# Two pieces of w1 asked for ahead of the first keys and values, instead of four, and two converted ahead of the first maximum, instead of three

## The chip, the cores and the metric

The kernel runs on one core of a Trainium2 chip. The core has five engines with queues of their own: TensorE (PE in the profile, its weight loads PEld), VectorE (DVE), ScalarE (ACT), GpSimd (POOL) and SyncE (SP, which here only asks for transfers). Transfers run on 16 DMA engines. The metric is the time of one execution on the device, in microseconds (us).

## What is computed

Block-sparse attention for 4 batches, 8 heads, 768 positions of 64 dimensions, and behind it a normalised feed-forward layer with a residual:

```
block, n_blocks = 32, 24
scores = scale * q @ k.T                       # per batch and head
mask: own block and its two neighbours, first and last block (as row or column), 3 sampled blocks a row
attn = softmax(where(mask, scores, -1e9)); attn_out = attn @ v
x = attn_out, heads side by side               # (4, 768, 512)
xn = (x - mean) / sqrt(var + 1e-6) * g_ln
out = x + relu(xn @ w_ch1) @ w_ch2             # 512 -> 2048 -> 512
```

The weights come in as bits of 64-bit floats. The kernel turns them into 32-bit floats with integer operations and then into pairs of 16-bit floats (high and low part).

## The kernel before

**Tiles, jobs, visits.** The rows of a batch are six tiles of 128 rows, taken in the order 1, 2, 3, 0, 4, 5. A job loads the keys and values of a tile (tile 0, which holds the edge blocks, has two jobs). Each job has visits: two for an ordinary tile, one for each half of the heads. Keys (`ks`) and values (`vs`) have two buffers each, used in turn by the jobs.

**Steps.** The program is written out step by step, and each engine runs its instructions in the order in which they are written. Step s holds the scores and the maxima of visit s (`scores`, `biggest`), the product with the values and the evictions of visit s - 1 (`attn_v`, `evict`), the exponentials of visit s (`softmax`), and a list of tasks: the transposes (`turn`), the loads of the next job at a job's first visit (`keys`, `values`), and whatever `at(step, ...)` has put there. The feed-forward layer (`ffn`) begins in step 4, spread between the tasks.

**Transfers.** SP asks for the small inputs, the queries, the keys and the part of the values that needs no gathering. Job 0's keys are one transfer for windows (L144) and twelve for sampled blocks (L153), which need the block ids in registers first. GpSimd asks for the gathered values (L192, four for an ordinary tile), for the weights (L413 for w1, L416 for w2) and for the outputs. It also copies the edge keys (L168). SP's requests reuse eight completion semaphores in turn, so that a request can wait for an earlier one's landing.

**Weights.** w1 comes in eight pieces, w2 in sixteen. A piece of w1 lands in one of four places, `raw1`, which lie in the storage of w2's results (`w2h`, `w2l`). `split_w1` converts it: three integer instructions on VectorE (L421, L423, L425) into one of four places `con1` (`stg0`, `stg1`, the ends of `hh` and `hl`), two on ScalarE (L433, L434), and the subtraction for the low part on GpSimd (L435). Behind the subtraction of pieces 0 to 3, GpSimd asks for pieces 4 to 7. `split_w2` and `low_w2` do the like for w2 from step 3 on, four pieces a step. The first w2 pieces land in the places that pieces 6 and 7 of w1 were converted in, so their request waits for those.

```
    def split_w1(i):
        split_w(raw1[i % 4], con1[i % 4], w1h[:, :, fs], w1l[:, :, fs], SW1)
...
        if i + 4 < 8:
            load_w1(i + 4, nc.gpsimd)
```

Of the kernel before, what the change touches and what calls it, by code (L numbers as in the profile page):

```python
# [25 lines left out]
def sparse_attention_moe(  # L26
# [13 lines left out]
    nc = tc.nc  # L40
# [132 lines left out]
    def values(job):  # L173
        src, vs = v[job.b], job.vs
        if job.kind == "D":
            nc.sync.dma_start(vs[:, 0:6, :], src[0 : 6 * P, :].rearrange("(c p) e -> p c e", p=P))
            return
        n = len(job.blocks)
        i0 = job.blocks[0]
        nc.sync.dma_start(vs[0:96, 1 : 2 * n : 2, :],  # L180
                          bass.AP(src.tensor, src.offset + (i0 - 1) * BLK * HV,
                                  [[HV, 96], [BLK * HV, n], [1, HV]]))
        runs = [(0, n, NB - 1)]
        if NB - 2 in job.blocks:
            k = job.blocks.index(NB - 2)
            runs = [(0, k, NB - 1), (k, k + 1, NB)]
        for lo, hi, blk in runs:
            nc.sync.dma_start(vs[96:128, 2 * lo + 1 : 2 * hi : 2, :],
                              bass.AP(src.tensor, src.offset + blk * BLK * HV,
                                      [[HV, BLK], [0, hi - lo], [1, HV]]))  # L190
        for gg, i in enumerate(job.blocks):
            nc.gpsimd.indirect_dma_start(  # L192
                out=vs[:, 2 * gg, :], out_offset=None, in_=src,
                in_offset=bass.IndirectOffsetOnAxis(ap=rows[:, i : i + 1], axis=0))
# [217 lines left out]
    def load_w1(i, dma):  # L412
        dma.dma_start(raw1[i % 4].bitcast(I32), w1[i].bitcast(I32))  # L413
# [23 lines left out]
    def split_w1(i):  # L437
        fs = slice(i * 256, (i + 1) * 256)
        split_w(raw1[i % 4], con1[i % 4], w1h[:, :, fs], w1l[:, :, fs], SW1)
        split[1, i] = s  # L440
        if i + 4 < 8:
            load_w1(i + 4, nc.gpsimd)
# [56 lines left out]
    def at(step, fn, *args):  # L499
        todo.setdefault(step, []).append((fn, args))  # L500
# [4 lines left out]
    nc.scalar.dma_start(bid, blocks)  # L505
    nc.scalar.dma_start(id_sb, eye)
    nc.scalar.dma_start(g_sb, g.to_broadcast([P, DM]))
    for i in range(4):
        load_w1(i, nc.gpsimd)
    nc.vector.memset(eps, 1e-6)  # L510
    nc.vector.memset(rf, 0.0)
# [2 lines left out]
        pass  # L514
    index_b()
    values(jobs[0])
    for i in range(3):
        split_w1(i)
    for i in range(3, 8):
        at((i - 3) // 2, split_w1, i)  # L520
    for i in range(4):
        at(2, load_w2, i, nc.gpsimd)
    for i in range(16):
# [132 lines left out]
```

## Time and profile before

| | |
|---|---|
| median of 3 runs | 779.08 us (777.71 to 780.2) |
| the profiled execution | 781.21 us |
| its span, first to last instruction | 779.3 us |
| TensorE busy | 702.4 us, 90% |
| VectorE busy | 326.2 us, 42% |
| ScalarE busy | 271.9 us, 35% |
| GpSimd busy | 188.1 us, 24% |
| mean granted clock of TensorE, of full speed | 0.965 |
| moved by DMA | 132.16 MB, 170 GB/s in the mean |

The shares are means over a program with a beginning that is unlike the rest. In the page's forty slices of 19.5 us each, TensorE's busy tenths run 0445767 and stay at 9 from there to the last but one, while the DMA tenths run 8989872 in the first seven. Times below are counted from the span's start.

### The profile page before, as it was taken

The page shows a single profiled execution, that of the slowest core. Times are in us where ns is not written, and L with a number is a line of the kernel's source. Part 1 is how long each engine was busy: PE and PEld are TensorE (multiplying, and loading weights), DVE is VectorE, ACT ScalarE, POOL GpSimd, SP SyncE. Part 2 cuts the span into 40 slices and gives each one's busy share as a digit, 9 for nine tenths or more (in the row PEclk, how much of TensorE's full clock was granted, in tenths as well). Part 3 has the DMA queues.
Part 4 walks back from the last instruction along what each step waited for, and adds up shares of the span by engine and source line. Part 5 has one row for each costly group of instructions (what it writes and reads, how often), then busy time and mean ns, then how long its engine had stood idle before and what let it go on. Part 6 is the DMA issues. An engine that isn't in the chain of part 4 may idle for free.

```text
span 779.3 us, 21817 instructions
## 1 busy us (share of the span) xinstructions
PE 702.4 (90%) x9344; PEld 475.1 (61%) x9344; DVE 326.2 (42%) x658; ACT 271.9 (35%) x561; POOL 188.1 (24%) x220
## 2 busy tenths in 40 slices
PE   0445767999999999999999999999999999999997
PEld 0122653775775775865875856765856857757764
DVE  7577887343351333443432323444332333432211
ACT  2355344343342331443341523343423423342200
POOL 5565211133322203113421103115221012210000
PEclk9967877999999999999999999999999999999999
DMA  8989872767947355569855437379864247431000
GB/s 330 341 251 282 285 247 84 219 184 209 246 131 188 94 167 150 155 165 238 231 153 137 126 129 218 111 194 252 214 167 132 64 147 223 147 87 29 14 29 14
DMA packets 109792, 132.16 MB, mean 170 GB/s; under 512 B 34560, under 2 KB 80896, under 8 KB 108672
## 3 DMA queue, kind: packets, MB, share of 16 engines
q1 hardware_dynamic: 96848, 83.92, 40.5%
q0 software_dynamic: 12416, 46.51, 17.9%
q8 instruction: 74, 1.21, 0.7%
q10 hardware_dynamic: 432, 0.34, 0.1%
q14 instruction: 22, 0.18, 0.1%
HBM read 118.15 MB, written 6.29 MB: 160 GB/s over the span
## 4 chain that ended last, share of the span: by engine, by line
PE 71%; issue 13%; DMA 8%; DVE 5%; POOL 1%; SPq 1%; ACT 1%; POOLq 0%; DVEq 0%
PE pu L367 27%; PE pd L392 25%; PE ps L203 7%; PE pv L274 7%; PE pt L264 6%; DMA ks<-kT 5%; DMA vs<-v 3%; DVE ot L423 1%; DVE w2l L445 1%; DVE ot L421 1%; DMA samp<-sampled 1%; POOL xl L344 0%; DVE st L239 0%; DVE ot L425 0%; SPq L149 0%
## 5 line engine op out<-in xcount | busy, mean ns | idle before, releaser
L367 PEld LDWEIGHTS <-w1h 128*128 128x128 f16 x1664 | 153.6, 99 | 18.1 <-issue 0.2
L252 ACT ACTIVATE p<-ps,st 128x256 f32<-128x256 f32 (+1 forms) x208 | 85.9, 491 | 222.8 <-DVE rs L316 116.4
L392 PE MATMUL pd<-w2h,hl 128*128 128x512 f16 x384 | 147.0, 383 | 0.0
L392 PE MATMUL pd<-w2l,hh 128*128 128x512 f16 x384 | 147.0, 383 | 0.0
L392 PE MATMUL pd<-w2h,hh 128*128 128x512 f16 x384 | 146.9, 383 | 0.0
L378 DVE SCALAR_TENSOR_TENSOR hl<-pu,hh 128x512 f16<-128x512 f32 x96 | 66.4, 692 | 171.2 <-ACT hh L377 170.7
L392 PEld LDWEIGHTS <-hh 128*128 128x128 f16 x768 | 75.2, 99 | 84.7 <-issue 3.0
L367 PE MATMUL pu<-xth,w1h 128*128 128x256 f16 (+1 forms) x832 | 120.9, 267 | 0.0
L367 PE MATMUL pu<-xth,w1l 128*128 128x256 f16 (+1 forms) x832 | 120.9, 267 | 0.0
L367 PE MATMUL pu<-xtl,w1h 128*128 128x256 f16 (+1 forms) x832 | 120.8, 267 | 0.0
L203 PE MATMUL ps<-ks,q 64*32 64x256 f32 (+1 forms) x1664 | 73.5, 418 | 40.3 <-DMA ks<-kT 37.6
L239 DVE TENSOR_REDUCE st<-ps 128x4 f32<-128x1024 f32 (+1 forms) x60 | 69.0, 1151 | 93.5 <-PE ps L203 93.4
L192 POOL DMA_INDIRECT vs<-v,rows x88 | 86.9, 987 | 88.0 <-PE pv L274 49.4
L377 ACT ACTIVATE hh<-pu 128x512 f16<-128x512 f32 x96 | 57.5, 599 | 108.9 <-PE pu L367 108.5
L264 PE MATMUL pt<-id_sb,p 128*128 128x128 f32 x448 | 66.3, 289 | 27.3 <-ACT p L252 23.3
L398 DVE SCALAR_TENSOR_TENSOR ot<-pd,x 128x512 f32<-128x512 f32 x24 | 16.6, 690 | 160.3 <-PE pd L392 160.3
L367 PEld LDWEIGHTS <-w1l 128*128 128x128 f16 x832 | 78.5, 99 | 8.2
L265 ACT COPY pt<-pt 128x512 f32<-128x512 f32 x120 | 61.9, 564 | 61.2 <-PE pt L264 50.7
L264 PEld LDWEIGHTS pt<-id_sb,p 128*128 128x128 f32 x448 | 53.6, 147 | 39.2 <-ACT p L252 28.0
L274 PEld LDWEIGHTS pv<-vs,pt 128*32 128x32 f32 x3584 | 55.6, 110 | 33.9 <-issue 28.4
L400 POOL DMA_DIRECT2D out<-ot x24 | 14.0, 583 | 255.9 <-DVE ot L398 255.9
L203 PEld LDWEIGHTS ps<-ks,q 64*32 64x32 f32 x1664 | 27.1, 109 | 72.0 <-issue 37.1
(83 smaller groups left out, 454.0 us busy)
## 6 DMA issues: line engine op xcount, KB each, us to landing
ks<-kT SPq DMA_DIRECT2D x28, 768.0 KB
ks<-kT SPq DMA_DIRECT2D x264, 64.0 KB
vs<-v SPq DMA_DIRECT2D x20, 780.0 KB
vs<-v SPq DMA_DIRECT2D x4, 1560.0 KB
q<-qT SPq DMA_DIRECT2D x24, 256.0 KB
out<-ot POOLq DMA_DIRECT2D x24, 256.0 KB
vs<-v SPq DMA_DIRECT2D x16, 260.0 KB
w2h<-w POOLq DMA_DIRECT2D x4, 1024.0 KB
```

Source lines behind the costliest of these rows:

```text
L192: nc.gpsimd.indirect_dma_start(out=vs[:, 2 * gg, :], out_offset=None, in_=src, in_offset=bass.IndirectOffsetOnAxis(ap=rows[:, i : i + 1], ...
L203: nc.tensor.matmul(ps[32 * part : 32 * part + 32, col : col + n], lhs[64 * row : 64 * row + 64], rhs[64 * row : 64 * row + 64], start=True ...
L239: nc.vector.tensor_reduce(out=st[:, 0:n], in_=seen(vi), axis=AX.X, op=ALU.max, negate=True)
L252: nc.scalar.activation(p_s[:, h * w : (h + 1) * w], seen(vi)[:, h, :], AF.Exp, bias=vi.st[:, 4 + h : 5 + h], scale=0.125)
L264: nc.tensor.transpose(pt[:, k - lo, :], p_s[:, k * P : (k + 1) * P], id_sb)
L265: nc.scalar.copy(dst[:, lo:hi, :], pt[:, 0 : hi - lo, :])
L274: nc.tensor.matmul(pv[32 * row : 32 * row + 32, 65 * col : 65 * col + 65], pt[:, ch, 32 * row : 32 * row + 32], vs[:, vv, 65 * e : 65 * e ...
L367: nc.tensor.matmul(ph[:, j * n : (j + 1) * n], w[:, ct, fs], x[:, ct, 0:n], start=m == 0, stop=m == 3 * CT - 1, skip_group_check=True)
L377: nc.scalar.activation(dh, ph, AF.Relu)
L378: nc.vector.scalar_tensor_tensor(out=dl, in0=ph, scalar=0.0, in1=dh, op0=ALU.max, op1=ALU.subtract)
L392: nc.tensor.matmul(po, x[:, f, ts], w[:, f, :], start=m == 0, stop=m == 3 * FT - 1)
L398: nc.vector.scalar_tensor_tensor(out=ot, in0=po, scalar=1.0 / (SW1 * SW2), in1=t.x, op0=ALU.mult, op1=ALU.add)
```

## The change

Of the four pieces of w1 that GpSimd asked for first of all, it now asks for two there and for the other two behind the loads of job 0's values. Two pieces are converted ahead of step 0 instead of three, and the conversions of pieces 2 to 7 are spread as 2, 3 in step 0, 4, 5 in step 1 and 6, 7 in step 2, where they were 3, 4 in step 0, 5, 6 in step 1 and 7 in step 2.

```
-    for i in range(4):
+    for i in range(2):
         load_w1(i, nc.gpsimd)
     nc.vector.memset(eps, 1e-6)
     nc.vector.memset(rf, 0.0)
...
     index_b()
     values(jobs[0])
-    for i in range(3):
+    for i in range(2, 4):
+        load_w1(i, nc.gpsimd)
+    for i in range(2):
         split_w1(i)
-    for i in range(3, 8):
-        at((i - 3) // 2, split_w1, i)
+    for i in range(2, 8):
+        at((i - 2) // 2, split_w1, i)
```

On GpSimd, at the program's start: `L413` asks for a piece of w1, `L168` copies edge keys into job 0's buffer, `L192` gathers job 0's values, `L435` is the subtraction of a piece.

```order
 L413 DMA w2h<-w 128x2048 x2
-L413 DMA w2l<-w 128x2048 x2
 L168 COPY ks_79<-kg_81 128x4x128 x2
 L192 DMA vs_83<-v,rows 128x520 x4
+L413 DMA w2l<-w 128x2048 x2
 L435 ISA
 L435 TENSOR_TENSOR w1l<-stg_108,w1h 128x4x256
```

The requests for pieces 2 and 3 went behind the four gathers of job 0's values. The rows of SP's queue are the same as before.

On VectorE, between step 1 and step 2: the three rows on `hh` are piece 6, those on `stg_109` ahead of them end piece 5; `L239` and `L240` are the maxima of the third visit, `L316` to `L322` the evictions of the second.

```order
 L425 SCALAR_TENSOR_TENSOR stg_109<-w2h,stg_109 128x1024
+L239 TENSOR_REDUCE st_417<-ps_400 128x4
+L240 TENSOR_SCALAR st_417<-st_417 128x4
+L316 TENSOR_SCALAR rs_453<-pv_420 128x4
+L318 RECIPROCAL rs_453<-rs_453 128x4
+L322 TENSOR_TENSOR x_90<-pv_420,rs_453 128x256
 L421 TENSOR_SCALAR hh<-w2l 128x1024
 L423 SCALAR_TENSOR_TENSOR hh<-w2l,hh 128x1024
 L425 SCALAR_TENSOR_TENSOR hh<-w2l,hh 128x1024
-L239 TENSOR_REDUCE st_423<-ps_406 128x4
-L240 TENSOR_SCALAR st_423<-st_423 128x4
```

Piece 6 went from ahead of the third maxima to behind the second visit's evictions; piece 7 (on `hl`) follows it there.

On GpSimd at the same place: `L435` on `hh` and `hl` are the subtractions of pieces 6 and 7, `L168` and `L192` belong to job 2, and `L416` is the first request for w2.

```order
 L435 TENSOR_TENSOR w1l<-stg_109,w1h 128x4x256
-L435 TENSOR_TENSOR w1l<-hh,w1h 128x4x256
 L168 COPY ks_79<-kg_81 128x4x128 x2
 L192 DMA vs_83<-v,rows 128x520 x4
+L435 TENSOR_TENSOR w1l<-hh,w1h 128x4x256
 L435 TENSOR_TENSOR w1l<-hl,w1h 128x4x256
 L416 DMA hh<-w 128x1024
```

Piece 6's subtraction went behind job 2's copies and gathers, next to piece 7's.

## Rows read from the trace of the kernel before

**Rows 1.** Busy us by stretch: PE, PEld, DVE, ACT, POOL, clock, DMA share, GB/s.
```profile
4.00:28.00 24.00, 2.70 (x12) 0.64 (x12) 18.84 (x33) 6.30 (x6) 12.75 (x11) 1.00 1.03 392
28.00:49.00 21.00, 8.90 (x132) 5.36 (x132) 15.90 (x18) 10.21 (x17) 12.01 (x11) 0.84 1.07 295
49.00:60.00 11.00, 6.55 (x109) 3.11 (x111) 5.69 (x9) 5.51 (x9) 8.14 (x6) 0.68 0.68 217
...
72.00:132.00 60.00, 38.74 (x611) 27.29 (x611) 51.97 (x92) 23.13 (x46) 10.42 (x17) 0.78 0.71 221
132.00:779.00 647.00, 638.39 (x8373) 434.97 (x8373) 226.95 (x496) 218.25 (x471) 134.85 (x160) 0.99 0.54 150
```
**Rows 2.** TensorE's waits, 80 to 140 us: total us, times, longest.
```profile
PE pt L264 <- ACT p L252: 17.5, 3, 9.2
```
**Rows 3.** Timeline of VectorE: start, us, line, tiles, idle before and its releaser.
```profile
32.72 1.23 DVE L239 TENSOR_REDUCE st<-ps 128x4 f32<-128x1024 f32 x1 [8.25 <-PE ps L203]
...
48.11 0.69 DVE L421 TENSOR_SCALAR hh<-w2l 128x1024 int32<-128x1024 int32 x1
...
48.83 1.23 DVE L423 SCALAR_TENSOR_TENSOR hh<-w2l,hh 128x1024 int32<-128x1024 int32 x1
...
50.09 1.23 DVE L425 SCALAR_TENSOR_TENSOR hh<-w2l,hh 128x1024 int32<-128x1024 int32 x1
...
58.53 0.68 DVE L421 TENSOR_SCALAR hl<-w2l 128x1024 int32<-128x1024 int32 x1
...
72.14 0.43 DVE L421 TENSOR_SCALAR ot<-hh 128x512 int32<-128x512 int32 x1 [5.13 <-DMA hh<-w]
```
**Rows 4.** The chain of waits, 0 to 84 us: start, us, what.
```profile
28.29 21.23 DMA vs<-v
...
52.41 4.01 PE ps L203 x32
```
**Rows 5.** Timeline of GpSimd.
```profile
2.53 1.06 POOL L413 DMA_DIRECT2D w2l<-w  x2
...
15.92 0.95 POOL L192 DMA_INDIRECT vs<-v,rows  x1 [0.30 <-issue]
...
42.35 0.59 POOL L413 DMA_DIRECT2D w2l<-w  x1
...
64.12 2.13 POOL L435 TENSOR_TENSOR w1l<-hl,w1h 128x1024 f16<-128x1024 f32 x1 [1.49 <-ACT w1h L434]
...
66.19 0.59 POOL L416 DMA_DIRECT2D hh<-w  x1
```
**Rows 6.** The page's DMA requests: count and KB of each.
```profile
ks<-kT SPq DMA_DIRECT2D x28, 768.0 KB
...
vs<-v SPq DMA_DIRECT2D x20, 780.0 KB
...
w2h<-w POOLq DMA_DIRECT2D x4, 1024.0 KB
```
**Rows 7.** DMA queues, 12 to 16 us (q0 GpSimd's, q1 SP's): packets, MB, share.
```profile
q0 software_dynamic: 187, 1.40, 82.8%
q1 hardware_dynamic: 189, 0.29, 19.2%
```
**Rows 8.** DMA queues, 28 to 32 us.
```profile
q1 hardware_dynamic: 588, 0.99, 105.5%
```
**Rows 9.** DMA queues, 36 to 40 us.
```profile
q0 software_dynamic: 263, 1.16, 73.1%
q1 hardware_dynamic: 269, 0.41, 28.4%
```
**Rows 10.** Timeline of TensorE: the scores of visit 0, last wait for keys.
```profile
30.00 1.92 PE L203 MATMUL ps<-ks,q 64*32 64x256 f32 x20 [2.47 <-DMA ks<-kT]
```
**Rows 11.** DMA queues, 48 to 50 us.
```profile
q0 software_dynamic: 90, 0.74, 91.6%
q1 hardware_dynamic: 104, 0.06, 11.6%
```

## The prediction

> **What bounds the kernel now.** I read the busy shares by stretch first, then the chain of waits of the first 84 us, then engine timelines around the places of the change, and last the DMA queues. [rows 1] split the program in two. From 132 us TensorE is busy 638.39 of 647.00 us: nothing that the change touches runs there, so a shift at 132 us arrives at the end as it is. From 72 to 132 us VectorE is busy 51.97 of 60.00 us, converting w2 in the order of its queue, and TensorE waits for it each step: three waits of the transposes for the exponentials cost 17.5 us [rows 2]. So a shift of the first w2 conversion, which starts at 72.14 us after 5.13 us of waiting for its transfer [rows 3], passes through as well. Before 60 us no engine is full, but the DMA share is 1.03 from 4 to 28 us and 1.07 from 28 to 49 us [rows 1]: the transfers are the bound. The chain [rows 4] names which: job 1's values, asked for at 28.29 us, are the last thing to land, 21.23 us later at 49.52 us. Their landing lets SP ask for the last of job 1's keys (its requests reuse completion semaphores, so one waits for an earlier one), and then come the scores of the third visit, until 56.42 us.
>
> So the time of the end is, in order: job 1's last key; the scores behind it; VectorE's third maximum and the second visit's evictions; the conversions of w1 queued behind those; the first w2 transfer; the w2 conversions. I call the first of these T, and ask two things: how far T moves, and what moves between T and 72.14 us.
>
> **First part: pieces 2 and 3 leave the front of the queue.** Before, GpSimd asks for the third and fourth piece at 2.53 us; the change puts them behind the indirect loads of job 0's values, whose last is asked for at 15.92 us and takes 0.95 us [rows 5]; so they are asked for at about 17. A piece is 1,024 KB, 1.05 MB [rows 6]. What a piece costs the keys is seen in the queue rows. From 12 to 16 us GpSimd's queue moved 187 packets and 1.40 MB, SP's 189 packets and 0.29 MB [rows 7]: packet for packet, so SP, whose rows are short, gets 0.07 MB per us beside 0.35. Alone SP moves 0.99 MB in 4 us, 0.25 per us [rows 8]. Beside a mixture with the indirect loads, whose rows are short too, it is 0.41 against 1.16 MB in 4 us, 0.10 and 0.29 per us [rows 9].
>
> With these rates I lay out the queues anew (an estimate from the rows named). Two pieces, 2.1 MB at 0.35, are through 6 us after the first packets at some 4 to 5 us; I take 11 us. Up to job 0's last key SP has to move 2.04 MB (72, 128 and 256 KB of small inputs, 768 KB of keys [rows 6], and twelve blocks of 128x128 floats, 64 KB each); some 0.6 are done by 11 us. The four indirect loads (each 128 rows of 520 floats, 1.06 MB together) take 3.7 us at 0.29, with 0.37 MB of SP's beside them; the other 1.1 MB go at 0.25, in 4.3 us. Job 0's keys are in at 19 us, where TensorE's last wait for them now ends at 30.00 us [rows 10]. That is 11 us, but not 11 us of T: VectorE's 8.25 us of waiting before the first maximum [rows 3] disappear with it, and nothing on the path hangs on either.
>
> From 19 us SP has to move job 0's values, the next queries, job 1's edge and window keys and its values: 2 x 1.065 + 0.262 + 0.786 = 3.18 MB, with 780 KB and 768 KB from [rows 6], the rest from the shapes. GpSimd's queue has pieces 2 to 5 (4.2 MB at 0.35: until 31), job 1's indirect loads (1.06 at 0.29: until 34.7), pieces 6 and 7 (2.1 at 0.35: until 40.7; VectorE has converted pieces 2 and 3, 3.2 us each, by about 29, so they are asked for in time). In these 21.7 us SP gets 18 x 0.07 + 3.7 x 0.10 = 1.63 MB; the other 1.55 go alone, in 6.2 us. Job 1's values land at 46.9 us instead of 49.5: **-2.6 us**.
>
> Behind them comes a tail of small keys. It now runs into piece 7, asked for at 42.35 us [rows 5], of which 90 packets and 0.74 MB pass between 48 and 50 us while the keys get 0.06 MB [rows 11]. In the new layout piece 7 is through by then. Those 2 us moved 0.06 MB of SP's, which alone take 0.3 us; but the last five requests are paced by their own issue, so I take **-1.0** of the possible 1.7. T moves by -3.6 us.
>
> Bounds for T. At one end every byte that stood ahead of T still does, and the share is already full: 0. At the other, the 21 us from 28 to 49 run at 295 GB/s where those before run at 392 [rows 1], because SP's queue is then mostly alone. If all of it ran mixed at 392, the stretch would shrink by 21 x (1 - 295/392) = 5.2 us, with 1.7 for the tail: -6.9. I take -3.6, since the layout still has SP alone for 6 us.
>
> The Trainium skill (DMA: Bandwidth & Descriptors, "Issuing engines are not separate DMA queues") says that requests of all engines run on the same 16 DMA engines and interleave. By that rule alone, on a share of 1.0, reordering would give T nothing; the 295 against 392 GB/s of this trace say that the mixture matters.
>
> **Second part: conversions move by half a step.** Pieces 2 to 6 change places with the maxima. For pieces 2 to 5 this costs nothing: they end before T, under VectorE's waits for keys, and in the new layout all four are done by about 37 us. Piece 6 is different. Now it is converted in step 1, ahead of the third maximum: 48.11, 48.83 and 50.09 us, 3.2 us from start to end on VectorE [rows 3], wholly under the wait for job 1's keys. Afterwards it stands in step 2, behind the evictions that follow those keys and ahead of piece 7, which starts at 58.53 us now [rows 3]. Queued behind it are piece 7, the norm, the fourth maximum; on GpSimd, piece 7's subtraction at 64.12 us and, at 66.19 us, the request for the first piece of w2 [rows 5], for which VectorE waits until 72.14. ScalarE and GpSimd take 2.1 us for a piece each and follow VectorE, so each of these is late by VectorE's 3.2 us. The transfer itself, 5.95 us from request to first use, I leave as it is: it gets clear of some of job 2's keys, and runs into the transposes instead. **+3.2 us**, from 2.2 (a quicker transfer) to 4.2 (the transposes and GpSimd beside VectorE). The norm and its transposes are late by 3.2 us too, but are used only after job 2's scores; job 2's keys have less beside them and are earlier. The w2 conversions still stand ahead of the fifth maximum on VectorE, so earlier keys give nothing back there.
>
> **Sum.** -2.6 - 1.0 + 3.2 = -0.4 us. The profiled execution took 781.21 us, span 779.3 and 1.9 around it; it would become 780.8. The median of the runs shown is 779.08, 2.1 lower; the same step from there gives **778.7 us**.
>
> **Rivals.** A measurement of this kernel can tell about 0.3% from no change, 2.3 us; below, "same" is 776.7 to 781.4.
>
> Slower: T does not move, because the 16 engines are full from 4 to 49 us and pieces 6 and 7 now pass entirely ahead of job 1's values. For it: shares of 1.03 and 1.07. Against it: the two rates of [rows 1]. Then only the 3.2 us of piece 6 are left: 782.3 us. It decides from the point where T gains less than 0.9 us. Chance 0.22. The skill's rule above leads here.
>
> Faster by mixing: job 1's values run beside the weights at more than 0.07 MB per us, as SP did with 0.10 in [rows 9]; T moves by up to 6.9 and the end by -3.7: 775.4 us. For it: the rate of values beside w1 rows is not in this trace, which has only keys there. Against it: one packet for one in every mixed window. Chance 0.16.
>
> Faster by cover: piece 6 is hidden after all, because the w2 transfer is quicker by as much once job 2's keys are through. Then -3.6 stands alone: 775.5 us. For it: VectorE waits 5.13 us for that transfer now. Against it: the request itself is late, behind piece 7 on GpSimd. Chance 0.10.
>
> The forecast, a gain of T eaten by piece 6, has 0.52, with its own range from 776.7 to 781.4. Faster is 0.16 + 0.10 = 0.26, slower 0.22. The range takes in most of both sides: 775.3 to 782.5.
>
> **What would show it.** TensorE's last wait for job 0's keys ends near 19 us and the first maximum starts near 21. The chain's transfer of job 1's values ends near 47, and the third visit's scores end near 53 instead of 56.42. Piece 6's three instructions stand behind the second visit's evictions, about 55 us, with piece 7 after them. The first w2 request is at about 66 and its first conversion within 1 us of 72.14. Everything behind keeps its distances. The prediction is wrong if job 1's values land at 49 or later, or before 45, or if the distance from the third scores to the first w2 conversion (15.7 us now) grows by less than 2 or more than 4.5 us.

## The result and the profile after

| | before | after |
|---|---|---|
| median | 779.08 us | 784.84 us (783.58 to 786.39, 5 runs) |
| ratio, 95% interval | | 1.0068 [1.0051, 1.0086] |
| the profiled execution, its span | 781.21, 779.3 us | 785.08, 783.2 us |
| TensorE, VectorE, ScalarE, GpSimd busy | 702.4, 326.2, 271.9, 188.1 us | 700.0, 322.4, 272.2, 188.6 us |
| mean granted clock | 0.965 | 0.954 |

The kernel became slower by 0.68%, 5.3 us. 778.7 us was forecast, with a range to 782.5: the forecast was wrong. No engine has noticeably more to do (the largest rise is 0.5 us, on GpSimd), so the time is waiting.

Busy time by stretch of the changed kernel, with the columns of [rows 1]:

```profile
4.00:28.00 24.00, 6.96 (x48) 3.03 (x56) 13.18 (x32) 6.67 (x10) 16.04 (x17) 1.00 1.03 319
28.00:49.00 21.00, 4.67 (x104) 2.94 (x88) 16.95 (x17) 11.37 (x15) 10.98 (x8) 0.61 1.03 357
49.00:60.00 11.00, 2.86 (x25) 0.96 (x30) 0.00 (x0) 0.00 (x0) 2.73 (x3) 0.50 0.68 170
72.00:132.00 60.00, 37.62 (x553) 27.23 (x553) 48.51 (x85) 25.84 (x51) 16.59 (x24) 0.76 0.77 252
132.00:783.00 651.00, 640.88 (x8455) 436.22 (x8447) 233.94 (x510) 221.10 (x476) 134.62 (x160) 0.99 0.54 149
```

Read the last two columns. The DMA engines are about as full as before, with a share of 1.03 in both stretches (1.03 and 1.07 before), but from 4 to 28 us they carry 319 GB/s where they carried 392, and from 28 to 49 us 357 where it carried 295. What the mixture (both queues moving at once) gives in the second stretch, the first has lost. Then comes a stretch, 49 to 60 us, in which VectorE does nothing at all.

The chain of waits of the changed kernel, from 2 to 80 us (start, us, what):

```profile
2.20 11.72 DMA ks<-kT
14.97 5.24 DMA ks<-kT
20.22 34.07 DMA vs<-v
...
56.83 2.58 DMA ks<-kT
59.54 1.92 PE ps L203 x20
...
64.16 0.77 DVE hh L421
64.95 1.34 DVE hh L423
66.32 1.24 DVE hh L425
...
75.12 3.78 DMA hh<-w
79.00 0.44 DVE ot L421
```

Job 1's values are asked for 8 us earlier than in [rows 4], and land at 20.22 + 34.07 = 54.29 us, 4.8 later than the 49.52 there. The last keys follow, and the third visit's scores end at 61.46 (56.42 before). Then piece 6, on `hh`, is on the chain itself. VectorE's timeline around it (with the columns of [rows 3]):

```profile
61.49 1.23 DVE L239 TENSOR_REDUCE st<-ps 128x4 f32<-128x1024 f32 x1 [15.29 <-PE ps L203]
...
64.16 0.76 DVE L421 TENSOR_SCALAR hh<-w2l 128x1024 int32<-128x1024 int32 x1
...
67.46 0.69 DVE L421 TENSOR_SCALAR hl<-w2l 128x1024 int32<-128x1024 int32 x1
...
79.00 0.43 DVE L421 TENSOR_SCALAR ot<-hh 128x512 int32<-128x512 int32 x1 [3.06 <-DMA hh<-w]
```

VectorE idles 15.29 us ahead of the third maximum. Piece 6 then takes it from 64.16 to 67.46, 3.3 us in which the conversions of piece 7 wait, and the first w2 conversion starts at 79.00 instead of 72.14 [rows 3].

### The profile page after: what moved, and what is told of

It is laid out like the page before. It is cut to its first block, busy times and chain, and to the rows that moved or that the text cites. A ratio compares the mean times of both kernels' runs of the same rounds, so it can differ in the third digit from the quotient of the medians.

```text
span 783.2 us, 21817 instructions
## 1 busy us (share of the span) xinstructions
PE 700.0 (89%) x9344; PEld 474.7 (61%) x9344; DVE 322.4 (41%) x658; ACT 272.2 (35%) x561; POOL 188.6 (24%) x220
## 4 chain that ended last, share of the span: by engine, by line
PE 70%; issue 13%; DMA 7%; DVE 6%; POOL 1%; ACT 1%; SPq 0%; POOLq 0%; DVEq 0%; ACTq 0%
PE pu L367 27%; PE pd L392 25%; PE pv L274 6%; PE ps L203 6%; PE pt L264 6%; DMA vs<-v 4%; DMA ks<-kT 2%; DVE ot L423 1%; DVE w2l L445 1%; DVE ot L421 1%; DVE ot L425 1%; DVE st L239 1%; DMA hh<-w 0%; POOL xl L344 0%; ACT p L252 0%
## 5 line engine op out<-in xcount | busy, mean ns | idle before, releaser
L192 POOL DMA_INDIRECT vs<-v,rows x88 | 86.6, 984 | 99.0 <-PE pv L274 60.6
L239 DVE TENSOR_REDUCE st<-ps 128x4 f32<-128x1024 f32 (+1 forms) x60 | 69.0, 1150 | 97.7 <-PE ps L203 97.7
L264 PEld LDWEIGHTS pt<-id_sb,p 128*128 128x128 f32 x448 | 54.3, 148 | 49.0 <-ACT p L252 42.7
```

The lines of the kernel that those rows point to most:

```text
L192: nc.gpsimd.indirect_dma_start(out=vs[:, 2 * gg, :], out_offset=None, in_=src, in_offset=bass.IndirectOffsetOnAxis(ap=rows[:, i : i + 1], ...
L239: nc.vector.tensor_reduce(out=st[:, 0:n], in_=seen(vi), axis=AX.X, op=ALU.max, negate=True)
L264: nc.tensor.transpose(pt[:, k - lo, :], p_s[:, k * P : (k + 1) * P], id_sb)
```

## The experiments

Three marks are read from every trace: **T**, the end of the third visit's scores (the prediction's T is the landing of the last keys just ahead of them); **R**, GpSimd's first request for w2; **C**, VectorE's first conversion of w2. Ratios are against the kernel before on the same chip. A time with a ratio is a median, one without is a single execution; T, R and C always come from one profiled execution.

| version | time, us | ratio [95%] | T | R - T | C - R | C |
|---|---|---|---|---|---|---|
| before, profile shown | 781.21 | | 56.42 | 9.77 | 5.95 | 72.14 |
| before, again (e8) | 780.74 | | 60.15 | 10.42 | 4.30 | 74.87 |
| before, again (p1) | 778.84 | | 58.22 | 10.43 | 4.55 | 73.20 |
| before, again (p2) | 781.76 | | 60.48 | 10.38 | 5.53 | 76.39 |
| after, profile shown | 784.84 | 1.0068 [1.0051, 1.0086] | 61.46 | 13.66 | 3.88 | 79.00 |
| after, again (p1) | 787.65 | | 62.21 | 13.66 | 3.92 | 79.79 |
| after, again (p2) | 785.30 | | 60.88 | 13.66 | 4.79 | 79.33 |
| requests alone (e1) | 779.83 | 1.0011 [0.9997, 1.0025] | 59.98 | 10.43 | 5.28 | 75.69 |
| requests alone, again | 779.42 | | 59.86 | 10.16 | 4.29 | 74.31 |
| conversions alone (e2) | 781.16 | 1.0036 [1.0024, 1.0047] | 57.10 | 13.60 | 4.22 | 74.92 |
| conversions alone, again | 782.31 | | 56.40 | 13.62 | 4.28 | 74.30 |
| after, requests ahead of the gathers (e3) | 780.90 | 1.0024 [1.0012, 1.0036] | 57.78 | 13.69 | 4.01 | 75.48 |
| after, piece 6 back in step 1 (e4) | 782.11 | 1.0043 [1.0029, 1.0057] | 60.89 | 10.47 | 4.16 | 75.52 |
| after, pieces 6 and 7 asked for late (e5) | 785.14 | 1.0083 [1.0060, 1.0106] | 59.92 | 13.69 | 4.55 | 78.16 |
| before, piece 7 in step 1 too (e6) | 780.34 | 1.0016 [1.0004, 1.0027] | 60.01 | 8.08 | 7.69 | 75.78 |
| before, three asked for ahead (e7) | 779.86 | 1.0009 [0.9994, 1.0023] | 59.76 | 10.15 | 5.48 | 75.39 |
| before, piece 6 asked for late (e9) | 780.48 | 1.0026 [1.0016, 1.0036] | 55.80 | 14.30 | 4.84 | 74.94 |
| conversions alone, piece 6 back (e10) | 783.65 | 1.0058 [1.0045, 1.0072] | 56.34 | 17.47 | 4.05 | 77.86 |

**The two halves apart.** My theory behind the result was that each half costs something: the requests make T late, the conversions make R late. The rival was that one of them carries it all.

Requests alone:

```
-    for i in range(4):
+    for i in range(2):
...
     values(jobs[0])
+    for i in range(2, 4):
+        load_w1(i, nc.gpsimd)
     for i in range(3):
         split_w1(i)
```

> Only the requests move (two pieces ahead, two behind the gathers of job 0's values); the conversions stand as in the kernel before, piece 6 in step 1. Theory A (the late requests move T, the landing of job 1's last keys): the scores of the third visit end at 60 to 62 us as in the changed kernel (61.46), against 56.42 before, and the time is 781 to 783 us. Theory B (T is unharmed by the requests, the conversions cost the time): the scores end at 55 to 57 us and the time is 778 to 780 us.

Conversions alone:

```
-    for i in range(3):
+    for i in range(2):
         split_w1(i)
-    for i in range(3, 8):
-        at((i - 3) // 2, split_w1, i)
+    for i in range(2, 8):
+        at((i - 2) // 2, split_w1, i)
```

> Only the conversions move (two ahead of step 0, piece 6 in step 2); all four requests stand first. Theory A: the scores of the third visit end at 55 to 58 us, and only the prediction's 3.2 us of piece 6 are added: 781 to 783 us. Theory B: nearly the whole loss of the changed kernel, 784 to 786 us.

The conversions alone cost 0.36%, 2.8 us, and R - T is 13.6 us. The requests alone cost 0.11%, 0.9 us, which the interval does not tell from nothing, and R - T stays at 10.4. The rival falls: neither half carries the 5.3 us. The two sum to 3.7; the 1.6 left over is within the three intervals (some 1 us each way for each half, 1.4 for both). T does not add up so simply: it is 59.98 and 59.86 us with the requests alone, within the scatter of before (below), 57.10 and 56.40 with the conversions alone, and 60.88 to 62.21 with both. The requests for pieces 6 and 7 stand elsewhere in each: at 34.06 and 44.91 us in e1, at 42.66 and 45.33 in e2, at 37.25 and 39.92 in the changed kernel. What these two pieces do is tried below; that they make the difference between the halves and the whole is not shown.

**How far one profile can be trusted.** In e1 T was 59.98, 3.6 us later than in the profile of before, and yet the time hardly differed. Either the end does not follow T, or T of the profile of before was not a usual one. Both kernels were profiled again, with no edit.

> The kernel before once more, for a second profile: the third scores end at 56 to 57 us and the first output is converted at 139 us, as in the first profile; what lies between the first output and the end (634.8 us in the first profile, 631.3 in that of the changed kernel) shows whether that difference of 3.5 us belongs to the kernel or to the execution.

> The kernel before, a third profile. Two executions of it so far end the third scores at 56.42 and at 60.14 us. If the first was the rare one, this ends at 59 to 61; if the time of job 1's values is a matter of chance (whether they are through when piece 7 of w1 starts to move), the executions fall in two groups, 56 to 57 and 59 to 61.

> The changed kernel, a second profile. Theory A (the late requests move T in every execution): third scores end at 60.5 to 62.5 us, first output converted at 146 to 147. If its 61.46 us were chance, it can end at 57 to 59.

> The kernel before, a fourth profile: as for the third, in one of the two groups (56 to 57, 59 to 61).

> The changed kernel, a third profile: third scores end at 60.5 to 62.5 us by Theory A, first output at 146 to 147.

> The requests-only kernel once more: third scores at 59.5 to 62 us if the late requests always cost T, 82.5 to 83 us from there to the first output.

> The conversions-only kernel once more, for the scatter of T: third scores at 56.5 to 58.5 us if its late request for piece 6 settles T, anywhere from 56 to 60.5 if not; 85 us from there to the first output by either.

T of the kernel before scatters from 56.42 to 60.48 us in four executions; the profile on which the prediction was built holds the earliest, and the 56 to 57 us that were expected of the second profile did not come. That execution ends no earlier (781.21 us), since from C to the end of its span it took 707.2 us, where the other three took 703.4 to 703.9. After has 60.88 to 62.21 in three. In the means T moved from 58.8 to 61.5, **+2.7 us**, not the +5.0 that the two profiles shown would tell. With four and three executions and this scatter, such a mean is good to some 2 us (an estimate from the spread in the table). R - T moved from 10.25 to 13.66, +3.4, and C - R from 5.1 to 4.2, -0.9, together **+2.5**. Of these only R - T is clear of its scatter; C - R lies between 4.3 and 5.95 before and between 3.9 and 4.8 after. The mean of C moved from 74.2 to 79.4, +5.2, beside 5.3 us measured; that they agree so closely is in part luck.

**Why T is late: when pieces 2 and 3 are asked for.** The theory: behind the gathers the request comes too late to keep GpSimd's queue moving beside SP's from 12 to 24 us. The rival: asking for fewer pieces first is itself the loss, wherever the others stand. The changed kernel with the two requests moved from behind `values(jobs[0])` to ahead of it:

```
     index_b()
+    for i in range(2, 4):
+        load_w1(i, nc.gpsimd)
     values(jobs[0])
-    for i in range(2, 4):
-        load_w1(i, nc.gpsimd)
```

> The changed kernel with the requests for pieces 2 and 3 behind the copies of job 0's edge keys, but ahead of the gathers, so at about 7 us instead of 17. Theory A (what costs is that GpSimd's DMA queue runs empty from 11 us on and that the pieces come late): the stretch from 12 to 24 us moves about 390 GB/s as before, the third scores end at 55 to 58 us, and the time is that of the conversions alone, 781 to 783 us. If two pieces fewer at the very start were the cause, the time stays at 784 to 786 us.

Stretches of 4 us of the changed kernel, and then of this one (last two columns: DMA share, GB/s):

```profile
12.00:16.00 4.00, 1.21 (x8) 0.43 (x8) 3.93 (x4) 1.65 (x2) 3.11 (x3) 1.00 1.10 335
16.00:20.00 4.00, 1.52 (x7) 0.22 (x4) 1.38 (x2) 2.56 (x3) 3.93 (x4) 1.00 0.94 238
20.00:24.00 4.00, 1.92 (x20) 0.68 (x20) 0.43 (x1) 0.00 (x0) 4.00 (x5) 1.00 1.06 225
```

```profile
12.00:16.00 4.00, 0.00 (x0) 0.00 (x0) 3.93 (x4) 1.64 (x2) 3.10 (x3) 1.00 1.01 419
16.00:20.00 4.00, 0.00 (x0) 0.00 (x0) 1.38 (x2) 2.57 (x3) 3.84 (x4) 1.00 1.02 389
20.00:24.00 4.00, 1.00 (x8) 0.42 (x8) 0.00 (x0) 0.00 (x0) 3.83 (x5) 1.00 1.09 376
```

With the requests some 10 us earlier the stretch carries 419, 389 and 376 GB/s (before: 423, 386, 376), T is 57.78, near that of the conversions alone, and the ratio 1.0024, whose interval lies below that of the change. So asking for fewer pieces first is not the loss; asking for the other two late is. This one edit moves a second thing, though: with job 0's keys late again (TensorE's last wait for them ends at 32.07 us instead of 21.62), the conversions and with them the requests for pieces 6 and 7 are late too, at 43.63 and 46.30 us. What is due to which of the two, the run on these pieces below bounds. The sum over 12 to 24 us: 4 x (335 + 238 + 225) = 3.19 MB moved, 4.74 before; 1.55 MB less, 4 us at 392 GB/s. The other two profiles of after have 299 and 312 GB/s in these 12 us against 383 to 396 in the four of before, so 0.8 to 1.6 MB is the loss, at that rate 2 to 4 us.

One more point between the two, the kernel before with three pieces ahead and the fourth behind the gathers:

```
-    for i in range(4):
+    for i in range(3):
...
     values(jobs[0])
+    load_w1(3, nc.gpsimd)
```

> The kernel before with one piece, the fourth, asked for behind the gathers; the conversions as before. Theory A (GpSimd's DMA queue runs empty from 11 us on when two pieces are behind): with three ahead it is full until about 14 us, the stretch from 12 to 24 us moves 340 to 390 GB/s, the third scores end at 57 to 59 us, between 56.42 before and 60.0 with two pieces behind, and the time is 778 to 780 us. If any piece asked for at 17 us costs the whole, the scores end at 60 or later.

No difference that can be measured; T lies among those of before. One piece behind the gathers costs nothing that shows, and gives nothing.

**Why T is late: pieces 6 and 7.** In the changed kernel these are asked for at 37.25 and 39.92 us, so that they move beside job 1's values. The theory: put off until the values are nearly through, they leave T earlier. The rival: what waits is only moved. The changed kernel with this in `split_w1`:

```
-        if i + 4 < 8:
-            load_w1(i + 4, nc.gpsimd)
+        for k in {0: [4], 1: [5], 5: [6, 7]}.get(i, []):
+            load_w1(k, nc.gpsimd)
```

> The changed kernel, with pieces 6 and 7 asked for behind the subtraction of piece 5, in one go, instead of behind those of pieces 2 and 3: at about 50 us instead of 37 and 40. Theory A, second half (what delays T are the two pieces that now pass beside job 1's values): job 1's values land at 48 to 50 us (54.3 in the changed kernel) and the third scores end at 56 to 58.5 us instead of 61.46; pieces 6 and 7 land in the gap behind, and the time is 781 to 783 us. If the slow stretch from 12 to 24 us alone delays T, the scores end at 60 to 62 us and the time stays at 784 to 786 us.

Job 1's values landed at 48.14 us instead of 54.29, so these pieces do hold them up. But the gain ended at the next transfer. TensorE's timeline of this kernel:

```profile
58.00 1.92 PE L203 MATMUL ps<-ks,q 64*32 64x256 f32 x20 [6.08 <-DMA ks<-kT]
```

The last keys now wait 6 us beside the two pieces. T is 59.92 and the time no better. The values land as early here as in e3 (48.70 us), where the requests for pieces 2 and 3 are not late: so it is pieces 6 and 7 beside them, not the loss from 12 to 24 us, that hold the values back. T is 2.1 us later here than in e3, one execution each: no more than that is left for the late requests of pieces 2 and 3 themselves, and it is less than one kernel scatters. The same shows in e2, where the conversions' move puts these requests off to 42.7 and 45.3 us: there job 1's values land at 47.71, and the last keys take 6.23 us.

**Piece 6.** The theory: its 3.2 us are paid in full wherever it stands behind T. The rival: they are hidden by the w2 transfer. The changed kernel with piece 6 alone back in step 1:

```
-        at((i - 2) // 2, split_w1, i)
+        at((i - 2) // 2 if i != 6 else 1, split_w1, i)
```

> The changed kernel with piece 6 converted in step 1 again, all else as changed. If piece 6 behind the second evictions costs its 3.2 us of VectorE, the first w2 conversion starts at 75 to 77 us (79.0 in the changed kernel) and the time is 781 to 782.5 us; if it is hidden by the w2 transfer or the norm, the time stays at 784 to 786 us. The third scores end at 61 to 62 us by either.

Its VectorE timeline:

```profile
46.11 1.75 DVE L421 TENSOR_SCALAR hh<-w2l 128x1024 int32<-128x1024 int32 x1 [0.78 <-DMA w2l<-w]
...
60.93 1.22 DVE L239 TENSOR_REDUCE st<-ps 128x4 f32<-128x1024 f32 x1 [8.75 <-PE ps L203]
...
75.52 0.43 DVE L421 TENSOR_SCALAR ot<-hh 128x512 int32<-128x512 int32 x1 [3.35 <-DMA hh<-w]
```

T stays late, at 60.89, and R - T goes back to 10.47. Over all runs the distance is 13.6 to 13.7 us in the seven profiles with piece 6 behind the third maximum and 9.8 to 10.5 in the eight with it ahead and asked for as early as in before or after. The ratio fell from 1.0068 to 1.0043, though these two intervals overlap a little.

If a piece ahead of the third maximum is covered, piece 7 might be too. The kernel before with that (`at((i - 3) // 2 if i != 7 else 1, split_w1, i)`):

> The kernel before with piece 7 of w1 converted in step 1 as well, ahead of the third maxima: the opposite of what the change does to piece 6. If a conversion behind the second evictions delays the first w2 conversion by VectorE's 3.2 us, this takes 3.2 us out: the first w2 conversion starts at 68 to 70 us (72.14 before), the fifth maximum at 78 to 80 (81.4; bounded by job 2's scores), and the time is 775.5 to 777.5 us. If the wait for the w2 transfer hides it, or piece 7 lands too late and holds up the third maximum, the time is 778 to 780 us.

```profile
68.09 0.60 POOL L416 DMA_DIRECT2D hh<-w  x1
```

```profile
75.78 0.43 DVE L421 TENSOR_SCALAR ot<-hh 128x512 int32<-128x512 int32 x1 [6.93 <-DMA hh<-w]
```

The first fence is GpSimd's timeline, the second VectorE's. R - T falls to 8.08, and C - R rises to 7.69: the request now follows job 2's gathers at once and its transfer takes that much longer. No gain; the time is 0.16% above before.

The cover has a condition: the piece must have landed. Two runs make its request late. The kernel before with pieces 6 and 7 both asked for behind piece 3's subtraction (`{0: [4], 1: [5], 3: [6, 7]}` in `split_w1`):

> The kernel before, with piece 6 asked for together with piece 7 behind piece 3's subtraction (about 42 us instead of 29); conversions as before. If T hangs on whether job 1's values are through when weights move beside them, they land at 46 to 48 us here, the third scores end at 56.5 to 58 us in every execution (56.4, 58.2, 60.1 and 60.5 in the four of before), the distance from there to the first output stays at 82.5 to 83, and the time is 776.5 to 778.5 us against 778.8. If the weights then only hold up job 1's last keys instead, the scores end at 58.5 to 60.5 and the time is the same as before.

And e2 with piece 6 back in step 1, where its request is at 43.18 us:

> All four requests first, two conversions ahead of step 0, pieces 2 and 3 in step 0, 4 to 6 in step 1: the conversions-only kernel (ratio 1.0036) with piece 6 put back. If piece 6 behind the second evictions is the whole cost of the conversions, its 2.5 to 3 us go: third scores at 56.5 to 58.5, 82.5 to 83 us from there to the first output instead of 85.0, ratio 0.998 to 1.001. If the later places of pieces 2 and 4 cost as well, the ratio stays above 1.002.

VectorE's timeline of e10:

```profile
52.04 2.62 DVE L421 TENSOR_SCALAR hh<-w2l 128x1024 int32<-128x1024 int32 x1
54.69 3.03 DVE L423 SCALAR_TENSOR_TENSOR hh<-w2l,hh 128x1024 int32<-128x1024 int32 x1
57.76 1.23 DVE L425 SCALAR_TENSOR_TENSOR hh<-w2l,hh 128x1024 int32<-128x1024 int32 x1
58.90 1.22 DVE L239 TENSOR_REDUCE st<-ps 128x4 f32<-128x1024 f32 x1
```

And GpSimd's:

```profile
66.91 1.02 POOL L192 DMA_INDIRECT vs<-v,rows  x1 [0.16 <-DVE ln L336]
...
73.81 0.59 POOL L416 DMA_DIRECT2D hh<-w  x1
```

e9 has the earliest T of all, 55.80, and yet is 0.26% slower than before; e10 has T at 56.34 and is 0.58% slower. In e10 the scores end at 56.34 but their maximum starts at 58.90, because piece 6 is still being converted ahead of it. Its subtraction on GpSimd is ahead of job 2's gathers, which start at 66.91 us instead of 57.60 in the profile of before, whose T is nearly the same. In e9 the maximum is hardly held (it starts at 55.84 us), but the subtraction, at 57.23, stands ahead of the gathers all the same, and they start at 62.13. R - T is 14.30 in e9 and 17.47 in e10, against the 13.6 of a piece behind the maximum: a piece ahead of it that lands late costs R more than one behind it. In the time this shows for e10 alone (1.0058, with 1.0036 for e2).

No version was faster than the kernel before.

## Why the prediction was wrong, point by point

**The step that failed** is the one headed "First part": "Job 1's values land at 46.9 us instead of 49.5: -2.6 us", with "-1.0" for the tail behind it, "T moves by -3.6 us". Measured: the values land at 54.29 us (54.3 to 55.1 in the three executions), later than the 49 that the prediction itself named as a sign of being wrong, and T moved by +2.7 in the means (the landing of the last keys by +3.2). That is 6.3 us off, and more than the whole error of the sum. The mechanism named there, mixing, was real: 28 to 49 us went from 295 to 357 GB/s. What was wrong is the layout of the queues that fed it, at two places.

First, "GpSimd's queue has pieces 2 to 5 (4.2 MB at 0.35: until 31)" lets this queue run at 0.35 MB per us from 19 us. The DMA queues of the changed kernel, 18 to 21 us, then 21 to 24, then 42 to 50 (with the columns of [rows 7]):

```profile
q1 hardware_dynamic: 468, 0.65, 92.8%
q0 software_dynamic: 23, 0.06, 10.8%
...
q0 software_dynamic: 87, 0.37, 55.7%
q1 hardware_dynamic: 157, 0.31, 51.0%
...
q0 software_dynamic: 273, 2.00, 78.1%
q1 hardware_dynamic: 277, 0.54, 22.6%
```

Pieces 2 and 3 were asked for at 16.98 us, but GpSimd's queue moved 0.06 MB from 18 to 21 us and 0.12 per us from 21 to 24. The four gathers stood ahead of the pieces: from 11 to 21 us the queue moved 0.88 MB, and the gathers alone are 1.06. How long this lasts differs between executions. GpSimd's queue from 18 to 24 us in the profile shown and in the other two of the table (p1, p2):

```profile
q0 software_dynamic: 110, 0.43, 33.2%
...
q0 software_dynamic: 183, 1.11, 63.8%
...
q0 software_dynamic: 219, 1.36, 76.2%
```

Their T is 61.46, 62.21 and 60.88, so the near standstill of the first is not what makes T late. What all three share is that the queue is nearly empty from 11 to 14 us (0.05 to 0.07 MB, 1.05 before) and that it does not keep up the 0.35 of the layout: from 24 to 37 us it moves 0.27 to 0.31 MB per us in the mean. In the profile shown it turns to short rows, job 1's gathers, only from 37 to 42 us (333 packets, 1.15 MB); so pieces 2 to 5 are through at about 37 us instead of 31, and the gathers at about 42 instead of 34.7 (an estimate from these packets). e3 shows that the late requests of pieces 2 and 3, with all that follows from them, make T late (57.78 without them); e5 leaves at most some 2 us of this for what is not pieces 6 and 7.

Second, the layout has all of pieces 6 and 7 through by 40.7 us, while SP still has values to move alone. In the trace they are asked for at 37.25 and 39.92 us and pass from 42 to 50 us, packet for packet (273 against 277), at 0.25 MB per us, and job 1's values get 0.07. That rate of 0.07 was foreseen; that it would hold until 50 us was not. e5 shows that without them the values land 6 us earlier, and also that this is worth little, since the keys behind the values then wait instead.

That the 56.42 us of the profile were the earliest of four does not excuse the step, since T was forecast as a difference; it only makes the two profiles shown overstate the miss.

**What held.** "For pieces 2 to 5 this costs nothing", "+3.2 us" for piece 6: R - T grew by 3.4, and the conversion is seen on the chain. Of these, 0.9 in the means, no more than their scatter, came back through a quicker w2 transfer, which the prediction left as it was and whose lower bound (2.2) covers it: +2.5 up to C. The prediction said that the distance from the third scores to the first w2 conversion would grow by 2 to 4.5 us; it grew by 2.5 in the means (by 1.8 between the two profiles shown). What lies behind it passed through to the end, as the first paragraphs said: 5.2 at C, 5.3 in the time.

Job 0's keys came early, as foreseen, and were worth nothing, as foreseen. TensorE's last wait for them, 30.00 us in [rows 10], in the changed kernel (19 was predicted; the layout left out the 0.34 MB of small inputs that ScalarE, not SP, asks for):

```profile
21.62 1.92 PE L203 MATMUL ps<-ks,q 64*32 64x256 f32 x20 [2.77 <-DMA ks<-kT]
```

**The rivals.** "Slower: T does not move" had the right sign, from piece 6 alone: 782.3 us. It fell 2.5 us short of 784.84, because T did not stay but moved later. The rule of the Trainium skill named there (DMA: Bandwidth & Descriptors, "Issuing engines are not separate DMA queues") led to that rival. The interleaving shows in the 273 packets against 277, but the rows go beyond it: 28 to 49 us of the changed kernel, with a share of 1.03, carry 357 GB/s, and 12 to 24 us, with the same share, 266. "Faster by cover" has a small part of truth in the 0.9 us. "Faster by mixing" is refuted: job 1's values ran at 0.07 MB per us beside w1 from 42 to 50 us, not faster.

**What stays open.** The 1.6 us by which both halves together exceed their sum may be nothing. Why the late requests do not move T clear of the scatter when they stand alone, and seem to beside the moved conversions, was not settled, nor why T of one and the same kernel scatters by 4 us. Nor was it tried what makes GpSimd's requests start late.

## What to carry to other kernels

A transfer moved back from the front of a full queue pays only if the engines that it leaves are kept as busy by something else at once; compare the bytes moved stretch by stretch, not the time at which the first consumer gets its data. A conversion that stands under a wait costs its full length once it is put behind that wait, and stands there for nothing only if its data has landed. Take the marks on which a forecast of a few us rests from several profiles of the kernel before, or give them the scatter that one profile hides.

## What the runs showed of the hardware

Twice in the kernel before, GpSimd's queue moved next to nothing for some 5 us after a request, while SP's short rows filled the engines. It asks for piece 6 at 28.79 us and for piece 7 at 42.35; its DMA queues from 28 to 34 us, then from 42 to 47:

```profile
q1 hardware_dynamic: 816, 1.39, 105.0%
q0 software_dynamic: 10, 0.02, 1.1%
...
q1 hardware_dynamic: 846, 1.04, 108.8%
q0 software_dynamic: 13, 0.00, 0.2%
```

Five us after the first request its queue had moved 0.02 MB. The other three executions of this kernel show the same behind the request for piece 6, with at most 0.02 MB in some 5 us. Why is not shown.

A full share is not a rate: 1.03 went with 319, 357 and 392 GB/s in stretches of these two kernels.

TensorE's clock in the changed kernel was granted at 0.52 of full speed from 32 to 64 us, the lower of the levels 1.2 and 2.4 GHz for nearly all of it. From 4 to 28 us, at 1.00, TensorE had been busy for 6.96 us; in the 32 us at the low level it was for 9.38. The clock is no part of the loss that can be seen at the third scores: the group of 20 that ends them took 1.92 us at 59.54 (clock 0.50), and the like group of visit 0 took 1.92 at 21.62 (clock 1.00). In another execution of the changed kernel (p2) the clock was granted at 1.00 from 32 to 64 us, and T (60.88) and R - T (13.66) are like those of the other two.
